# VectorE's pieces at fixed places of the attention strings, copied score tiles and twelve projection pieces in the last 64 steps

## The chip, the cores and the metric

The kernel runs on one core of a Trainium2 chip. The metric is the device time of one execution in microseconds (us). Its engines are TensorE (PE; its weight loads are shown apart as PEld), VectorE (DVE), ScalarE (ACT), GpSimd (POOL) and SyncE (SP), which here only issues DMAs. Each works through its own instructions in program order and waits on semaphores for the others.

## The reference

Two layers, each an attention block and a Fourier block (FNet) with a residual around both. S = 2048 tokens, D = 640, H = 32 heads of 20.

```python
def _A_ref(x, wqkv, wo):
    qkv = (x @ wqkv).reshape(B, S, 3, H, Dh).transpose(2, 0, 3, 1, 4)
    q, k, v = qkv[0], qkv[1], qkv[2]
    p = softmax(einsum("bhqd,bhkd->bhqk", q, k) * Dh ** -0.5)
    o = einsum("bhqk,bhkd->bhqd", p, v)
    return o.transpose(0, 2, 1, 3).reshape(B, S, D) @ wo
def _B_ref(x, dft_seq_re, dft_seq_im, dft_hid_re, dft_hid_im):
    a = einsum("bsd,ed->bse", x, dft_hid_re); b = einsum("bsd,ed->bse", x, dft_hid_im)
    return einsum("ts,bse->bte", dft_seq_re, a) - einsum("ts,bse->bte", dft_seq_im, b)
x = A_x
for layer in (0, 1):
    x = x + _A_ref(layernorm(x), A_wqkv, A_wo)
    x = x + _B_ref(layernorm(x), dft_seq_re, dft_seq_im, dft_hid_re, dft_hid_im)
```

The four DFT matrices are inputs. The kernel uses their symmetries to do a fraction of the Fourier work, and therefore compares the matrices with these symmetries while it runs (the class Check). If the comparison fails, it does everything again in a general way that is not taken here.

## The kernel before, in words

**A layer's stages.** A prologue makes the first queries and keys and half of the values. The attention sweep follows: 512 steps. A step is one group of 4 heads, one block of 512 queries and one chunk of 128 keys; 16 steps in a row (kc = 0 to 15) share an accumulator. Then `Project.run` multiplies the attention's output o with wo, adds the residual and normalizes, and `Fourier.run` does the Fourier block.

**A step.** Two score tiles (`scores`, L666): two matmuls each, side by side on TensorE's rows, into one of three PSUM tiles of 128x1024 (`psc`). ScalarE takes the exponential of each tile into an SBUF tile `e` out of a ring of 7 (L674). Then `values` (L688) adds e times v to the accumulator `acc`. The trace lists a step as 4 matmuls of L666, 8 of L688 and 2 ACTIVATEs. A score tile can be *copied*: VectorE moves it to SBUF (L671, `e<-psc`), which frees the PSUM tile, and ScalarE takes the exponential later from SBUF in place (`e<-e`).

**Fill work on TensorE.** Beside the steps TensorE makes the queries, keys and values that later heads need, in blocks (`block`, 'f'), into one PSUM tile `fill`. VectorE then works on the result: `keep` rounds it to a high part (L275), subtracts it for the low part (L263), and keeps the largest squares (L271, L272); GpSimd stores both parts. `norm` ('n') is one small matmul over these squares (L301). When no such work is left, `block` takes pieces of the projection: `Project.begin` (L1208) does the first three fifths of half a token tile's product with wo, 9 matmuls of 128x320 (L99 to L101), and VectorE adds the residual (L1215). `Project.product` (L1223) leaves out what is begun. Before, five token tiles are begun, so ten pieces.

**The order** of all instructions is written out by strings, one letter at a time (`sweep`): s a score tile, d or D a copied one (after d the exponentials that are due come out first, after D they wait for the next s), v the values of a step, f a block, n a norm, h one piece of waiting VectorE work.
- Steps below 233: DENSE strings of 8 steps (two blocks, two copied tiles); while the second half of v is made (steps 128 to 191), 4-step strings without copies. Before, neither has an h.
- Steps 233 to 408: eleven LOOSE strings (`STRING`) of 16 steps, 11 copied tiles, 12 h and 3 blocks each. Here the ring has 3 more `ex` tiles (`widen`), and `keep`'s operations are put into the list `soon` (when `defer` is set) and taken out one by one at h.
- Steps 409 to 447: no string, no block.
- Steps 448 to 511: ten strings of 5 to 8 steps (`tail`), one block each, no copied tile.

**VectorE's other work.** After each 16 steps `finish` transposes the accumulator (L697), and five operations make o in two parts (L709 to L725), which GpSimd stores (L729). Outside of the LOOSE strings all five come out at once. `compare` hands out the tasks of Check: a load of 2 x 512 KB by GpSimd's queue (L1022) into the tiles c0 and c1, then reductions and differences on VectorE (`most`, L1027; `differ`, L1031). It spreads them over the steps, not counting the 176 LOOSE ones, so that they end near step 490, at most two per step, and those of a load not before 5 steps after it (`landed`). `tasks` are the loads and splits of wo and the hidden-DFT weights.

Of the kernel before, what the change touches and what calls it, by code (L numbers as in the profile page):

```python
# [25 lines left out]
NQ = NT // 4  # L26
# [16 lines left out]
def mha_fnet_kernel(ctx, tc, x_in, wqk, wv, wo, seq, hid, nat_seq, nat_hid, out):  # L43
# [530 lines left out]
    class Attention:  # L574
        THIN = 233
        LOOSE = range(THIN, THIN + 176, 16)
        STRING = "sDhsfsDshvvshDsvvshDsfDhsvvsDsvvsDsfshDshvhvsDsvvshDsvhhvsDsnvhv"

        def __init__(s, qkv, L):
            s.a = qkv  # L580
            s.k, s.q, s.e, s.held, s.soon, s.due = {}, {}, {}, [], [], {}
# [52 lines left out]

        def widen(s):
            x = s.a.fill("wv", [3, 2, 512], F32, "ex")
            s.extra = [lambda k=k: x[:, k] for k in range(3)]
            s.ring = s.extra + s.ring
            s.a.defer = s.soon

        def narrow(s):
            s.settle()
            s.ring = [f for f in s.ring if f not in s.extra]
            s.a.defer = None

        def settle(s):
            while s.soon:
                s.soon.pop(0)()
# [44 lines left out]
        def finish(s, g, qb):  # L693
            while s.a.defer is not None and s.held:
                s.held.pop(0)()
            t0 = s.room("ofsh", [16, 32], F32, "of")
            V.transpose(t0.rearrange("p b c -> p (b c)"), s.acc)  # L697
# [36 lines left out]
        def sweep(s, shift, begin, fill=lambda n: None, plan=None, block=None, compare=lambda n: None, norm=None):  # L734
            done = calm = n = 0

            def release():
                while s.held:
                    s.held.pop(0)()

# [12 lines left out]
            while n < len(s.steps):  # L753
                opened(n)
                order = plan and plan(n)
                if order:

                    while done < n - 1:
                        s.values(done)
                        done += 1  # L760
                    t, loose = 2 * n, n in s.LOOSE
                    for k, c in enumerate(order):
                        if c in "sdD":
                            m, j = divmod(t, 2)
# [33 lines left out]
                for _ in range(count):  # L798
                    s.values(done)
                    done += 1  # L800
            for n in range(done, len(s.steps)):
                s.values(n)
            release()

        def run(s, done, project, check):

            work, tasks, later = s.a.work(), s.a.vweights(1, s.a.fill, pause=[lambda: None] * 2), list(check)
            s.work, s.blocks, s.after, s.rest, s.more, s.landed = True, 0, None, 0, False, 0


            tail, n = {}, 448
            for steps in (6, 7, 6, 8, 6, 6, 6, 6, 5, 8):
                tail[n] = {5: "sssfssvssvvsssvv", 6: "sssfssvssvssvvsssvv", 7: "sssfssvssvssvssvvsssvv",
                           8: "sssfssvssvsvssvssvssvssvv"}[steps]
                n += steps

# [3 lines left out]
            def block(n):  # L820
                if not s.work:
                    project.parts.pop(0)()
                    return
                if not s.more:
                    norm(n)
                    s.settle()
                try:
                    f = next(work)
                    s.blocks += 1
                    s.more = f is True  # L830
                    s.after = (n + (2 if n < s.THIN else 4), f) if f and not s.more else None
                    s.rest = s.after[0] + 2 if s.after else n
                except StopIteration:
                    s.work = False
                    tasks.extend(done())
# [18 lines left out]
            def plan(n):  # L854
                if n in tail:
                    return tail[n]
                if n == s.LOOSE[0]:
                    s.widen()
                if n == s.LOOSE[-1] + 16:
# [9 lines left out]
            def compare(n):  # L869


                if n < 8:
                    return
                for _ in range(2):
                    if not later or n < s.landed or (len(check) - len(later)) * (490 - len(s.LOOSE) * 16) >= (
                            n if n < s.THIN else n - len(s.LOOSE) * 16) * len(check):
# [5 lines left out]
                    task()  # L882

# [31 lines left out]
        def general(s, done, project):  # L915
# [6 lines left out]
            for f in done():  # L922
                f()
            mx = s.room("c0", [2, NT, H], F32, "mx")[:, 0]
# [38 lines left out]
    class Check:  # L963
# [65 lines left out]
        def differ(s, to, x, y, op):  # L1029

            V.tensor_tensor(y, x, y, op=op)  # L1031
            s.most(to, y)

        def compare(s, n):
# [37 lines left out]
            def hid_first():  # L1072
                t = s.t[n]
                if m:
                    for k, x in enumerate((lolo, hilo, hihi)):
                        s.most(own[0:1, k + 1:k + 2], t[x][0:1])
                s.differ(own[0:1, 0:1], t[hilo][0:1, 1:], t[hihi][0:1, 1:], same)

# [25 lines left out]
            if is_seq:  # L1104
                def halves():
                    x = s.t[n][lolo]
                    s.differ(far[:p, 4:5], x[:, 0:256], x[:, 256:512], OP.subtract if (m == 0) == (j < NQ) else OP.add)
                out.append(halves)
# [13 lines left out]
        def compare_middle(s, m):  # L1122
# [15 lines left out]
            def rest():  # L1138
                x = s.t["mid"][:, 0]
                s.differ(far[:, 1:2], x[:, :256], x[:, 256:], same)  # L1140
                s.differ(far[:, 4:5], x[:, :128], x[:, 128:256], same)

# [25 lines left out]
    class Project:  # L1168
        def __init__(s, att, src, dst):
# [3 lines left out]

            s.begun, s.parts = set(), [lambda n=n, i=i: s.begin(n, i) for n in range(5) for i in range(2)]
            s.early = {474: [lambda: s.fetch(0, 0, 1)], 486: [lambda: s.fetch(1, 0, 0)], 503: [lambda: s.fetch(0, 1, 1)]}

        def weights(s, dc):
# [5 lines left out]

            return load, lambda: split(s.w[dc][:, 0], s.w[dc][:, 1], s.raw[dc], vector=True)

# [22 lines left out]
        def begin(s, n, i):  # L1208
# [157 lines left out]
    class Fourier:  # L1366
# [9 lines left out]
        def weights(s, k):  # L1376
# [10 lines left out]
            def parts():  # L1387
                w, d = s.w[ri, c], s.deep(ri, c)
                split(w[:d, 0], w[:d, 1], s.raw["w", k][:d], vector=True)

# [305 lines left out]
    def layer(start, src, dst, general, tasks, after):  # L1696
# [14 lines left out]
        def done():  # L1711
# [11 lines left out]
            def along(k, *fs):  # L1723
                first = out[k]
                out[k] = lambda: [f() for f in (first, *fs)]
# [147 lines left out]
```

## Time and profile before

| | us |
|---|---|
| median of 3 runs | 2408.72 (2408.35 to 2409.49) |
| the profiled execution | 2408.86 |
| its span, first to last instruction | 2407.0 |
| layer 0: first score to step 448 | 82.2 to 962.4 |
| layer 0: step 448 to the first projection product of `Project.run` | 962.4 to 1085.97 |
| layer 0: the products of `Project.run` | 1085.97 to 1143.26 |
| layer 1: the same three | 1275.9 to 2157.4, to 2279.96, to 2337.25 |

All times in the views are us from the first instruction. In a view by windows each engine has its busy time, with the number of instructions that begin in the window in brackets. In a list of waits stand the total, the number of times and the longest. In a timeline row x4 means four instructions merged; what stands in square brackets is the idle time before them and what ended it.

### The profile page before, as it was taken

To read this page: it belongs to the slowest core of one execution; us is meant where nothing else is said; L and a number is where in the kernel's file an instruction comes from. 1 tells how busy PE (TensorE), PEld (TensorE's weight loads), DVE (VectorE), ACT (ScalarE), POOL (GpSimd) and SP (SyncE) were. 2 spreads that over 40 slices of the span, in tenths; PEclk is the share of its full clock that TensorE was granted. 3 is DMA by queue.
4 is the path that set the end of the run, shared out by engine and by line. 5 is a ranking of instruction groups with operands and counts; after the bars stand their busy time and mean duration, and the time that the engine had idled before them with its cause. 6 is when DMAs were issued, how large, how long until landed. Compare 5 with 4: busy or idle time off the path is not lost. (4 is left out here: it accounts for less than half of the span.)

```text
span 2407.0 us, 44028 instructions
## 1 busy us (share of the span) xinstructions
PE 2379.7 (99%) x16200; PEld 1168.9 (49%) x16200; DVE 1393.2 (58%) x2654; ACT 2091.0 (87%) x2402; POOL 553.1 (23%) x1080
## 2 busy tenths in 40 slices
PE   9999999999999999999999999999999999999998
PEld 8644445544333332339885444454443333333496
DVE  7355664367666664527774766543566666644275
ACT  5799998899999999995357999988999999999852
POOL 3022221122111112215341122211211111223143
PEclk9999999999999999999999999999999999999999
DMA  6445342223121225319673343422221212243195
GB/s 210 134 155 169 125 134 67 94 93 103 56 76 55 71 79 166 116 53 322 236 237 112 109 146 104 138 72 59 71 85 52 85 50 70 76 145 90 51 324 213
DMA packets 136704, 289.02 MB, mean 120 GB/s; under 512 B 31628, under 2 KB 56108, under 8 KB 136480
## 3 DMA queue, kind: packets, MB, share of 16 engines
q1 hardware_dynamic: 93408, 171.07, 21.9%
q0 software_dynamic: 43072, 115.06, 14.9%
q8 instruction: 130, 2.13, 0.4%
q14 instruction: 94, 0.77, 0.1%
HBM read 187.38 MB, written 92.70 MB: 116 GB/s over the span
## 5 line engine op out<-in xcount | busy, mean ns | idle before, releaser
L674 ACT ACTIVATE e<-psc 128x1024 f32<-128x1024 f32 x1586 | 1554.5, 1117 | 89.2 <-PE psc L666 87.7
L688 PE MATMUL acc<-e,v 128*32 128x512 f32 x7336 | 946.9, 599 | 1.5 <-DVE of L697 1.4
L666 PE MATMUL psc<-stq,stk 62*128 62x512 f32 x4096 | 714.4, 440 | 6.1 <-ACT e L674 3.8
L666 PEld LDWEIGHTS psc<-stq,stk 62*128 62x128 f32 x4096 | 333.3, 184 | 631.0 <-ACT e L674 408.1
L671 DVE COPY e<-psc 128x1024 f32<-128x1024 f32 x248 | 303.3, 1223 | 349.6 <-PE psc L666 331.7
L688 PEld LDWEIGHTS acc<-e,v 128*32 128x32 f32 x7336 | 204.7, 109 | 378.4 <-issue 329.5
L106 PE MATMUL pqk<-xt,wqk 128*128 128x512 f32 x1200 | 321.1, 408 | 2.9 <-DVE xt L94 0.9
L674 ACT ACTIVATE e<-e 128x1024 f32<-128x1024 f32 x248 | 302.8, 1221 | 5.0 <-DVE e L671 4.8
L729 POOL DMA_DIRECT2D o<-oh x256 | 131.7, 522 | 701.0 <-DVE oh L722 673.2
L106 PEld LDWEIGHTS pqk<-xt,wqk 128*128 128x128 f32 x1200 | 214.2, 189 | 95.7 <-issue 44.9
L674 ACT ACTIVATE ex<-psc 128x1024 f32<-128x1024 f32 x136 | 163.0, 1256 | 1.3 <-PE psc L666 1.3
L106 PE MATMUL pv<-wv,xt 128*128 128x320 f32 x960 | 151.7, 313 | 0.0
L106 PEld LDWEIGHTS pv<-wv,xt 128*128 128x128 f32 x960 | 141.0, 188 | 13.7 <-issue 10.2
L688 PE MATMUL acc<-ex,v 128*32 128x512 f32 x856 | 145.7, 598 | 0.0
L729 POOL DMA_DIRECT2D o<-ot x256 | 128.4, 508 | 16.5 <-DVE ot L725 14.5
L671 DVE COPY ex<-psc 128x1024 f32<-128x1024 f32 x78 | 95.5, 1225 | 56.5 <-PE psc L666 51.0
L697 DVE STREAM_TRANSPOSE of<-acc 128x512 f32<-128x512 f32 x64 | 45.7, 715 | 127.4 <-PE acc L688 127.4
L1027 DVE TENSOR_REDUCE far<-cq 128x1 f32<-128x512 f32 (+5 forms) x169 | 98.5, 584 | 5.7
L674 ACT ACTIVATE ex<-ex 128x1024 f32<-128x1024 f32 x78 | 101.2, 1297 | 0.0
L99 PE MATMUL py<-wo,o 128*128 128x320 f32 x320 | 101.0, 316 | 0.0
L1031 DVE TENSOR_TENSOR cq<-cq 128x512 f32<-128x512 f32 (+4 forms) x166 | 96.6, 582 | 5.7 <-DMA cq<-in_nat_seq_dram 5.6
L260 POOL DMA_DIRECT2D scrq<-hl x40 | 28.5, 713 | 310.3 <-DVE hl L263 237.3
(226 smaller groups left out, 2092.4 us busy)
## 6 DMA issues: line engine op xcount, KB each, us to landing
cq<-in_nat_seq_dram POOLq DMA_DIRECT2D x64, 512.0 KB, 5.5
scrq<-hl POOLq DMA_DIRECT2D x40, 512.0 KB, 4.0
scrk<-hl POOLq DMA_DIRECT2D x40, 512.0 KB, 3.1
stq<-scrq SPq DMA_DIRECT2D x256, 80.0 KB
stk<-scrk SPq DMA_DIRECT2D x128, 160.0 KB
chl<-matrix SPq DMA_DIRECT2D x32, 512.0 KB
o<-o SPq DMA_DIRECT2D x32, 384.0 KB
stq<-scrq SPq DMA_DIRECT2D x256, 40.0 KB
```

What stands on the lines that cost most here:

```text
L99: PE.matmul(out_ap, ah, bh, start=start, stop=False)
L106: yield lambda i=i, j=j, k=k: PE.matmul(out_ap, a[i], b[j], start=dc == 0 and k == 0, stop=dc == ND - 1 and k == 2)
L260: G.dma_start(s.scr["qk"[k]][c * 128:(c + 1) * 128, :, tb * 512:(tb + 1) * 512], hl.bitcast(F32))
L666: PE.matmul(p[:, i], s.k[g, kc // 8, j][r, kc % 8 * 128:(kc % 8 + 1) * 128], s.q[g, qb, j][r], start=True, stop=True)
L671: V.tensor_copy(e, p)
L674: s.due[n, j] = lambda: A.activation(e, e if copied in ("d", "D") else p, AF.Exp, scale=SCALE)
L688: PE.matmul(s.acc[32 * j:32 * j + 32], s.a.v[kc][:, v0:v0 + 32], s.e[n, j // 2][:, j % 2], start=kc == 0, stop=kc == NT - 1, skip_group_ch ...
L697: V.transpose(t0.rearrange("p b c -> p (b c)"), s.acc)
L729: G.dma_start(s.o[k, h * DH:(h + 1) * DH, qb * 512:(qb + 1) * 512], hl[32 * j:32 * j + DH])
L1027: V.tensor_reduce(to, x, op=OP.max, axis=AX.X, apply_absolute_value=True)
L1031: V.tensor_tensor(y, x, y, op=op)
```

## The change

1. `keep`'s operations go through `soon` in the whole sweep (`defer` is set at its start), the five of `finish` through a list `ends`, and `step` (at h) takes one from `soon`, else `ends`, else `held`, else one task of `compare`. DENSE strings get 11 h each; their letters are otherwise the same. An operation of two instructions (a comparison's difference and its reduction, the split of a weight) returns its second one, which waits for the next h. Where no string with h runs, everything is emitted at once as before.
2. `compare` counts a LOOSE step as 0.15 of a step and ends at step 441 (`pace`). A load's tasks come 4 steps after it, not 5.
3. The last 64 steps are four ENDING strings of 16 steps, each with 11 copied tiles, 16 h and 3 blocks. The ring has two more tiles there, c0 and c1, which the comparison no longer needs.
4. Twelve projection pieces: token tiles 0, 1, 2, 3, 4 and 6. The residual rows of tiles 4 to 7 are loaded earlier among the `tasks`; three loads of o stand at other steps (`early`). VectorE's add after a piece goes through `soon`.

```diff
+    def halves(hl_h, hl_l, src):
+        V.tensor_copy(hl_h, src)
+        return lambda: V.tensor_tensor(hl_l, src, hl_h.bitcast(F32), op=OP.subtract)
...
+        LAST = range(448, 512, 16)
+        DENSE = "ssdfhhhsshsvvhssvvssdfhhhhsssvvhhssnvv"
+        ENDING = "sDsvDhhsfssdvhvssdhvhvsDhsfsDsvhhvsDsvhvsDhsvhvsDhsfsDsvhvhshDshvvv"
...
-        def step(s):
-            for todo in (s.soon, s.held):
+        def step(s, other):
+            for todo in (s.soon, s.ends, s.held, [other]):
                 if todo:
-                    todo.pop(0)()
+                    rest = todo.pop(0)()
+                    if callable(rest):
+                        s.held.insert(0, rest)
                     return
...
-            pieces = s.scaled(t0, g, qb)
-            if s.a.defer is None:
-                s.held.append(lambda: [f() for f in pieces])
-            else:
-                s.held += pieces
+            s.ends += s.scaled(t0, g, qb)
...
             def release():
+                s.settle()
+                s.settle(True)
                 while s.held:
-                    s.held.pop(0)()
+                    s.whole(s.held.pop(0))
...
-                    t, loose = 2 * n, n in s.LOOSE
+                    t, loose = 2 * n, "h" in order
...
-                            s.step()
+                            s.step(lambda: compare(t // 2 - 1, True))
...
+            s.a.defer = s.soon
-            tail, n = {}, 448
-            for steps in (6, 7, 6, 8, 6, 6, 6, 6, 5, 8):
-                tail[n] = {5: "sssfssvssvvsssvv", 6: "sssfssvssvssvvsssvv", 7: "sssfssvssvssvssvvsssvv",
-                           8: "sssfssvssvsvssvssvssvssvv"}[steps]
-                n += steps
...
-                if n in tail:
-                    return tail[n]
+                if n in s.LAST:
+                    if n == s.LAST[0]:
+                        assert not later
+                        s.widen([lambda k=k: s.room(f"c{k}", [2, 512], F32, "ec") for k in range(2)])
+                    return s.ENDING
...
-                    return "sssfsssvvssvv" if whole else "ssdfsssvvssvvssdfsssvvssnvv"
+                    return "sssfsssvvssvv" if whole else s.DENSE
...
+            def pace(n):
+                m = min(n, s.THIN)
+                n -= m
+                thin = min(n, len(s.LOOSE) * 16)
+                return m + 0.15 * thin + n - thin
...
-                        s.landed = n + 5
+                        s.landed = n + 4
...
             V.tensor_tensor(y, x, y, op=op)
-            s.most(to, y)
+            return lambda: s.most(to, y)
...
-            s.begun, s.parts = set(), [lambda n=n, i=i: s.begin(n, i) for n in range(5) for i in range(2)]
-            s.early = {474: [lambda: s.fetch(0, 0, 1)], 486: [lambda: s.fetch(1, 0, 0)], 503: [lambda: s.fetch(0, 1, 1)]}
+            s.begun, s.parts = set(), [lambda n=n, i=i: s.begin(n, i) for n in (0, 1, 2, 3, 4, 6) for i in range(2)]
+            s.early = {456: [lambda: s.fetch(1, 0, 0)], 482: [lambda: s.fetch(0, 0, 1)], 511: [lambda: s.fetch(0, 1, 1)]}
...
-            V.tensor_tensor(x, p, x, op=OP.add)
+            s.att.soon.append(lambda: V.tensor_tensor(x, p, x, op=OP.add))
...
-            for k, m in ((5, 0), (6, 1)):
+            for k, m in ((5, 0), (6, 1), (9, 2), (13, 3)):
                 along(k, lambda m=m: p.load(m))
-            out += [lambda: f.edges(0)] + [lambda k=k: p.load(k) for k in (2, 3)] + [lambda: f.edges(1)]
+            out += [lambda: f.edges(0), lambda: f.edges(1)]
```

More of the change, by code (lines that the diff above doesn't have):

```diff
@@ L633, in zeros, with widen @@
             nc.sync.dma_start(s.a.shift["b"][:, 1], z[:H].bitcast(F32))
-        def widen(s):
-            x = s.a.fill("wv", [3, 2, 512], F32, "ex")
-            s.extra = [lambda k=k: x[:, k] for k in range(3)]
+        def widen(s, extra):
+            s.extra = extra
             s.ring = s.extra + s.ring
-            s.a.defer = s.soon
         def narrow(s):
@@ L643, in narrow, with settle, whole @@
             s.ring = [f for f in s.ring if f not in s.extra]
[L644 to L648, printed above, removed]
-        def step(s):
-            for todo in (s.soon, s.held):
+        def settle(s, ends=False):
+            todo = s.ends if ends else s.soon
+            while todo:
+                todo.pop(0)()
+        @staticmethod
+        def whole(f):
+            rest = f()
+            if callable(rest):
+                rest()
+        def step(s, other):
+            for todo in (s.soon, s.ends, s.held, [other]):
                 if todo:
-                    todo.pop(0)()
+                    rest = todo.pop(0)()
+                    if callable(rest):
+                        s.held.insert(0, rest)
                     return
@@ L866, in plan, with compare @@
                 if n % 4 == 1 and n + (4 if whole else 8) <= s.THIN and (whole or s.blocks % 2 == 0):
-                    return "sssfsssvvssvv" if whole else "ssdfsssvvssvvssdfsssvvssnvv"
-            def compare(n):
+                    return "sssfsssvvssvv" if whole else s.DENSE
[4 more added lines that the diff above has]
+                return m + 0.15 * thin + n - thin
+            def compare(n, one=False):
                 if n < 8:
                     return
-                for _ in range(2):
-                    if not later or n < s.landed or (len(check) - len(later)) * (490 - len(s.LOOSE) * 16) >= (
-                            n if n < s.THIN else n - len(s.LOOSE) * 16) * len(check):
+                for _ in range(1 if one else 2):
+                    if not later or n < s.landed or (
+                            len(check) - len(later)) * pace(s.LAST[0] - 6) >= pace(n) * len(check):
                         break
@@ L879, in compare @@
                     if isinstance(task, tuple):
[L880 removed]
+                        s.landed = n + 4
                         task = task[1]
[L882 removed]
+                    if one:
+                        return task()
+                    s.whole(task)
             def need(n, *keys):
@@ L1724, in along, with both @@
                 first = out[k]
-                out[k] = lambda: [f() for f in (first, *fs)]
+                def both():
+                    rest = first()
+                    for f in fs:
+                        f()
+                    return rest
+                out[k] = both
             for k, m in ((1, 0), (3, 1)):
                 along(k, lambda m=m: p.fetch(0, m, 0))
-            for k, m in ((5, 0), (6, 1)):
+            for k, m in ((5, 0), (6, 1), (9, 2), (13, 3)):
                 along(k, lambda m=m: p.load(m))
-            out += [lambda: f.edges(0)] + [lambda k=k: p.load(k) for k in (2, 3)] + [lambda: f.edges(1)]
+            out += [lambda: f.edges(0), lambda: f.edges(1)]
             return out
```

24 lines of the change are left out of this document (13 added, 11 removed).

## The prediction

> **What bounds the kernel now.** I read the page first, then the sweep by windows at the borders of its stages, then waits, groups and timeline where the change touches them.
>
> ```profile
> span 2407.0 us, 44028 instructions
> ...
> PE 2379.7 (99%) x16200; PEld 1168.9 (49%) x16200; DVE 1393.2 (58%) x2654; ACT 2091.0 (87%) x2402; POOL 553.1 (23%) x1080
> ```
>
> ```profile
> 577.70:873.70 296.00, 295.37 (x2083) 115.09 (x2079) 198.75 (x262) 296.00 (x322) 51.26 (x97) 1.00 0.22 67
> 903.00:962.40 59.40, 59.39 (x396) 17.33 (x392) 26.72 (x65) 59.40 (x66) 14.10 (x24) 1.00 0.52 167
> 962.40:1085.97 123.57, 122.01 (x870) 47.33 (x866) 47.78 (x101) 119.22 (x129) 20.59 (x38) 1.00 0.28 85
> ...
> 2157.40:2279.96 122.56, 122.38 (x873) 47.45 (x869) 40.37 (x102) 119.11 (x129) 26.19 (x50) 1.00 0.23 64
> 1085.97:1143.26 57.29, 57.29 (x392) 57.29 (x391) 42.97 (x114) 28.70 (x57) 31.33 (x75) 1.00 0.97 334
> 2279.96:2337.25 57.29, 57.29 (x393) 57.29 (x392) 43.31 (x114) 28.59 (x57) 28.19 (x75) 1.00 0.96 334
> ```
>
> A window's columns are its length, the busy time of PE, PEld, DVE, ACT and POOL, the granted clock (1.00 everywhere, so it explains nothing), the share of the DMA engines and GB/s. The page says 99% PE, but a matmul that is spread out counts as busy too, so this names no bound. The stages do:
> - The first row holds ten LOOSE strings (steps 240 to 399). ACT is busy 296.00 of 296.00 us: **ACT bounds them**, at 296.00 / 320 = 0.925 us for an exponential, or 29.60 us for a string of 32.
> - In the sweep without blocks (second row) it is ACT again, 59.40 of 59.40.
> - The next two rows are the last 64 steps of each layer with what follows until the projection. ACT idles there for 123.57 - 119.22 = 4.35 us and for 122.56 - 119.11 = 3.45 us.
> - The last two are the products of the projection. PE and its weight loads fill all of it: **PE bounds it**, and each matmul taken out is a gain.
>
> **Twelve pieces instead of ten.** 2 x 9 = 18 matmuls of each layer go from the products into the sweep.
>
> ```profile
> 1085.97:1143.26 57.29, 57.29 (x390) 57.19 (x390) 13.76 (x62) 1.00 0.97 334
> ```
>
> ```profile
> L99 PE MATMUL py<-wo,o 128*128 128x320 f32 x130 | 40.2, 309 | 0.0
> ```
>
> The first row is the same window for the tile py alone: 390 matmuls in 57.29 us are 0.147 us each (the mean of 309 ns in the second row overlaps with the next). 18 x 0.147 = 2.65 us a layer, **5.3 us** for two. Next to be late would be the data, on DMA engines that are busy 0.97 of this time. I take nothing off, because the second row has no idle time before its 130 matmuls; it is a rival below. The three loads of o that move to steps 456, 482 and 511 go through SP's queue ahead of the projection's own loads. The last of them waits for o of the steps that end at 495, whose five operations the string has at its first six h, before its middle. I count the moved loads, and the two residual loads that come earlier, at nothing: in these 64 steps the DMA engines are busy 0.28 and 0.23 of the time, which covers them. Without that cover the projection would start late by one load.
>
> **The last 64 steps.** Four ENDING strings replace ten short ones. Like LOOSE each has 32 score tiles, 11 of them copied, and 16 values.
>
> ```profile
> L674 ACT ACTIVATE e<-psc 128x1024 f32<-128x1024 f32 x129 | 120.3, 1054 | 3.3 <-PE psc L666 3.3
> ```
>
> ```profile
> PE acc L688 <- DVE of L697: 1.4, 1, 1.4
> ```
>
> ```profile
> 1075.50 9.44 ACT L674 ACTIVATE e<-psc 128x1024 f32<-128x1024 f32 x10
> ...
> 1085.97 0.42 PE L99 MATMUL py<-wo,o 128*128 128x320 f32 x1
> ```
>
> In layer 0's 4.35 us of idle ACT, 3.3 wait for score tiles (first row), and PE itself waited 1.4 us once, because the transpose that frees the accumulator stood behind comparison work on DVE (second row). The rest comes after the last exponential, which ends at 1075.50 + 9.44 = 1084.94; the projection begins 1.03 us later (last two rows). This 1.03 us stays. If the copied tiles keep ACT full as in LOOSE, 4.35 + 3.45 - 2 x 1.03 = 5.7 us can go. Reading the copies costs ACT nothing new: 119.22 / 129 = 0.924 us for each now, against LOOSE's 0.925. Does the added fill fit?
>
> ```profile
> L106 PE MATMUL pqk<-xt,wqk 128*128 128x512 f32 x150 | 42.8, 415 | 0.0
> ...
> L671 DVE COPY e<-psc 128x1024 f32<-128x1024 f32 x76 | 93.0, 1224 | 60.7 <-PE psc L666 51.9 <-ACT e L674 4.4 <-ACT ex L674 4.1
> ```
>
> These are groups of the ten LOOSE strings: their blocks take 42.8 / 10 = 4.28 us of PE a string. An ENDING string has 27 x 0.147 = 3.97 us, so PE isn't worse off. On DVE 11 copies are 11 x 1.224 = 13.5 us of 29.6, which leaves 16 us for 16 h. The bounds of the unknown: 0 us, or 0.5 us a string (8 strings, 4 us) if the nine-tile ring and the longer letters leave gaps. LOOSE is nearer, so I take 0.1 a string: 5.7 - 0.8 = **4.9 us**.
>
> [...] Read by matmul occupancy (122.38 of 122.56), the 36 matmuls would lengthen these steps by the 5.3 us that they save later.
>
> **DENSE strings with fixed places.** Their letters for PE stay; DVE's work is spread.
>
> ```profile
> 245.20:277.50 32.30, 10.63 (x64) 5.07 (x64) 4.90 (x4) 26.48 (x29) 1.00 0.43 141
> 277.50:310.90 33.40, 10.75 (x64) 5.16 (x64) 4.86 (x4) 26.55 (x29) 1.00 0.36 113
> 1307.90:1341.50 33.60, 11.21 (x66) 5.14 (x66) 4.85 (x4) 26.49 (x29) 1.00 0.37 123
> 1341.50:1375.30 33.80, 10.66 (x66) 5.11 (x66) 4.86 (x4) 26.51 (x29) 1.00 0.36 117
> ```
>
> ```profile
> PE pn L301 <- DVE sq L272: 1.3, 2, 1.0
> PE psc L666 <- ACT e L674: 1.1, 2, 0.7
> PE pqk L106 <- DVE top L302: 0.8, 1, 0.8
> PE psc L666 <- DVE e L671: 0.6, 1, 0.6
> ```
>
> ```profile
> PE pn L301 <- DVE sq L272: 0.8, 1, 0.8
> ```
>
> ```profile
> 1341.66 0.41 DVE L271 TENSOR_TENSOR sqh<-hl 128x256 bf16<-128x256 f32 x1
> ...
> 1342.90 0.29 DVE L272 TENSOR_TENSOR sq<-sq,sqh 128x256 bf16<-128x256 bf16 x1
> ...
> 1343.24 0.38 PE L301 MATMUL pn<-sq,ind 128*32 128x512 bf16 x1 [1.02 <-DVE sq L272]
> ```
>
> The four windows are 16 steps each, for the score tile: 32.30 us undisturbed, up to 33.80 where PE waits. The first list of waits is of 1275 to 1540 us: DVE's part is 1.3 + 0.8 + 0.6 = 2.7 us in layer 1. In the last rows the norm stands 1.02 us because `sq` is made in one burst with what was queued before it. In layer 0 (82 to 345 us) there is one of 0.8, so 3.5 us in all are listed; by the windows, with the restart after a wait, it is up to 1.1 + 1.3 + 1.5 = 3.9 in these three alone. With 11 places in 8 steps, `keep`'s four pieces get the four h behind the second block and the five of `finish` come singly. Bounds: 0, if new waits take their place, and 5. I take **3.0 us**, most of the listed.
>
> **What the h bring into LOOSE, and the earlier landing.** Pieces of the comparison fill empty h, and its tasks come 4 steps after their load.
>
> ```profile
> 636.90:666.50 29.60, 29.51 (x214) 11.56 (x210) 21.01 (x29) 29.60 (x34) 5.32 (x10) 1.00 0.19 58
> 696.10:725.70 29.60, 29.54 (x213) 11.27 (x209) 19.53 (x26) 29.60 (x34) 5.18 (x10) 1.00 0.30 89
> ```
>
> ```profile
> DVE ctop L1027 <- DMA cq<-in_nat_seq_dram: 23.8, 9, 8.2
> ...
> DVE ctop L1027 <- DMA cq<-in_nat_hid_dram: 11.7, 4, 5.4
> ```
>
> ```profile
> cq<-in_nat_seq_dram POOLq DMA_DIRECT2D x64, 512.0 KB, 5.5
> ```
>
> A string with 21.01 us of DVE takes the 29.60 us of one with 19.53, so a piece or two more cost nothing there. A load is two DMAs with 5.5 us to landing; 4 steps are 4 x 29.60 / 16 = 7.4 us, so most land in time. DVE already waits for 13 of them, 35.5 us in all, and while it waits the copies behind it stand, PE behind the copies, ACT behind PE. One step less is 1.85 us more for those that are late. In LOOSE fall 0.15 x 176 = 26 of the 292 steps that the comparison counts (233 + 26 + 33), a tenth of its loads, some two a layer. If one in three is late, that is one or two waits in all; bounds 0 and 4 x 1.85 = 7.4 us. I take **0.7 us lost**. In steps 409 to 447 DVE is busy 26.72 of 59.40 us, so what the comparison has left finds room.
>
> **Sum.** 5.3 + 4.9 + 3.0 - 0.7 = 12.5 us. The profiled execution took 2408.86 us (span 2407.0), 0.14 above the median of 2408.72. 2408.7 - 12.5 = **2396.2 us**. A measurement of this kernel can tell about 0.2%, 4.8 us, from no change.
>
> **The rivals.**
> - *The last 64 steps keep their length* (chance 0.16). PE or the ring, not ACT, paces ENDING, at 0.5 us a string beyond LOOSE or more: 4.9 us shrink to about 0.9, so 2400.2. For it: PE's 122.38 of 122.56. [...]
> - *The projection is bound by DMA* (0.06). Its bytes are the same and the engines busy at 0.97; then the 5.3 us come back there as waits for o: 2401.5. Against: no product waits now, at 334 GB/s. [...]
> - *Slower: pieces push the copies in LOOSE* (0.11). If in each of the 22 strings one comparison operation comes ahead of a copy that is due and its whole time reaches ACT,
>
> ```profile
> L1031 DVE TENSOR_TENSOR cq<-cq 128x512 f32<-128x512 f32 (+4 forms) x166 | 96.6, 582 | 5.7 <-DMA cq<-in_nat_seq_dram 5.6
> ```
>
>   22 x 0.582 = 12.8 us eat the whole gain; two per string, or one with a landing of 1.85 us in every third string, make 22 x 1.16 = 25.6, so 2396.2 + 25.6 = 2421.8. It decides from 12.5 / 22 = 0.57 us a string. For it: ACT has no slack there at all. Against: the two windows with 21.01 and 19.53 us of DVE.
> - *The edit does little* (0.05). The h are taken by `keep`, `finish` and tasks, the bursts come at the next release, and the pieces wait for one another: 2407.
> - *More* (0.09): all DENSE waits go (5) and ENDING needs nothing extra (5.7): 2408.7 - 5.3 - 5.0 - 5.7 = 2392.7, or a little below.
>
> **How the numbers follow.** The forecast has 0.53, between 2393 and 2400. The range 2390 to 2406 takes in the first two rivals and More, and leaves out the slower one and the little one, 0.16, and some of the tails. Faster by over 0.2% means below 2403.9: the forecast, the first two rivals and More, less their upper tails: 0.77. Within 0.2%: those tails, the little one and the weak end of the slower one: 0.14. Slower: 0.09.
>
> **What would show it.** In the new profile: the products' window 2.65 us shorter, with 372 matmuls of py and no PE wait; from step 448's first score to the first product about 121 us, ACT idle for 1 to 2; DENSE windows near 32.3 to 32.7 throughout; LOOSE strings of 29.6. LOOSE at 30.2 or more, with DVE waiting for c tiles ahead of its copies, would prove me wrong, and so would ENDING strings over 30.1 or waits for o in the products.

## The result and the profile after

The changed kernel takes **2434.11 us** (median of 4 runs, 2431.74 to 2436.88), the kernel before 2408.88 on the same chip: a ratio of **1.0105**, 95% interval 1.0088 to 1.0123. The forecast was 2396.2 with a range from 2390 to 2406. The profiled execution took 2431.85 us, 23.1 us more span than before. The page of the changed kernel, whose rows are the span and the busy time of the engines:

```profile
span 2430.1 us, 44075 instructions
...
PE 2378.8 (98%) x16200; PEld 1173.3 (48%) x16200; DVE 1497.4 (62%) x2746; ACT 2090.8 (86%) x2402; POOL 554.5 (23%) x1080
```

Its windows, with the columns of the prediction's (length, busy PE, PEld, DVE, ACT, POOL, granted clock, DMA share, GB/s):

```profile
144.90:181.30 36.40, 34.49 (x230) 15.22 (x226) 17.89 (x29) 30.09 (x33) 6.05 (x13) 0.95 0.31 99
214.00:248.80 34.80, 32.88 (x227) 13.99 (x223) 18.27 (x34) 30.06 (x33) 8.33 (x16) 1.00 0.43 134
941.70:981.80 40.10, 32.04 (x206) 9.05 (x202) 17.02 (x42) 30.39 (x34) 6.10 (x11) 0.87 0.48 142
2148.60:2184.20 35.60, 32.31 (x206) 9.13 (x202) 14.55 (x43) 30.76 (x34) 13.08 (x24) 0.90 0.36 100
981.79:1102.48 120.69, 119.82 (x888) 50.97 (x884) 77.27 (x98) 119.19 (x129) 16.01 (x32) 1.00 0.21 56
2184.21:2304.92 120.71, 119.83 (x888) 50.95 (x885) 77.28 (x98) 118.83 (x129) 16.03 (x32) 1.00 0.21 57
1102.48:1157.14 54.66, 54.66 (x377) 54.66 (x373) 42.86 (x114) 27.84 (x57) 30.23 (x71) 1.00 0.98 342
585.80:615.40 29.60, 29.59 (x212) 11.57 (x208) 20.22 (x29) 29.60 (x33) 6.75 (x12) 1.00 0.38 119
```

Read them from below. A LOOSE string still takes 29.60 us with ACT at 100%. The products take 54.66 us instead of 57.29 (in layer 1, not shown, the same), and the last 64 steps 120.7 instead of 123.57 and 122.56. Three of the forecast's terms are there. The loss is in the first four rows: 16-step windows of DENSE (steps 32 and 64) at 36.40 and 34.80 us, and the last 16 steps before 448 at 40.10 in layer 0 and 35.60 in layer 1. What PE waited for says why. Its list for the changed kernel (total, times, longest):

```profile
PE pqk L111 <- DVE wqk L91: 14.3, 8, 1.8
PE acc L702 <- DVE of L710: 9.4, 2, 8.1
PE psc L680 <- ACT e L688: 3.9, 6, 0.8
PE pflag L1180 <- DVE cmax L1175: 3.3, 1, 3.3
```

The third stood there before, with 3.8. The other three are new or have grown (the one for the accumulator was 1.4), and all end on VectorE.

**The first loss: a weight's split behind a copied tile.** The timeline of the changed kernel at the border of two DENSE strings (start, length, engine, line, operation, and in square brackets the idle time before it):

```profile
145.56 0.39 PE L306 MATMUL pn<-sq,ind 128*32 128x512 bf16 x1
...
148.67 1.23 DVE L685 COPY e<-psc 128x1024 f32<-128x1024 f32 x1 [0.20 <-PE psc L680]
149.81 0.48 DVE L91 CAST wqk<-wraw 128x640 fp32r<-128x640 f32 x1
...
150.33 0.82 DVE L94 TENSOR_TENSOR wqk<-wraw,wqk 128x640 fp32r<-128x640 f32 x1
150.35 2.93 PE L111 MATMUL pqk<-xt,wqk 128*128 128x512 f32 x6 [1.79 <-DVE wqk L91]
```

The norm (145.56, the letter n) sets off the split of the weights that the next blocks need. That is a piece of VectorE work now, and it goes into `soon`. In DENSE no h stands behind n, so the piece waits for the next string and comes out at that string's f, directly ahead of the products that read it. By then the copy of the letter d (148.67) is queued on VectorE ahead of it. PE stands 1.79 us, four times in each layer.

**The second loss: the comparison comes too late to steps 409 to 447.** The DMA issues of its natural-order loads, by the line of the load, in the kernel before and in the changed one (number, shortest/median/longest ns, first and last start):

```profile
L1022 POOL DMA_DIRECT2D cq<-in_nat_seq_dram x64: 708/734/767, 262.9 to 1607.9; - x64
```

```profile
L1042 POOL DMA_DIRECT2D cq<-in_nat_seq_dram x64: 708/728/771, 376.5 to 1678.4; - x64
```

The first comes at 376.5 instead of 262.9 us. Counted from the kernel's own order of instructions, some 142 of 175 tasks are handed out by step 409 in layer 0 where 155 are due, and some 131 of 166 in layer 1 where 147 are due. The rest follows as fast as `landed` allows. In layer 0 five loads start between steps 409 and 448, at 903.2, 917.5, 927.9, 940.0 and 961.3 us. The timeline around the fourth, in the changed kernel:

```profile
940.00 1.44 POOL L1042 DMA_DIRECT2D cq<-in_nat_seq_dram  x2 [10.53 <-DVE bound L559]
...
948.19 0.69 DVE L1047 TENSOR_REDUCE ctop<-cq 128x1 f32<-128x512 f32 x1 [6.79 <-DMA cq<-in_nat_seq_dram]
...
953.56 0.70 DVE L710 STREAM_TRANSPOSE of<-acc 128x512 f32<-128x512 f32 x1
...
954.32 1.94 PE L702 MATMUL acc<-e,v 128*32 128x512 f32 x8 [8.06 <-DVE of L710]
```

The first reduction of the load comes 4 steps after it and stands 6.79 us on VectorE until the data land. Behind it in VectorE's queue are its own followers and then the transpose that frees the accumulator (953.56). PE waits 8.06 us for that. In layer 1 the last, small loads (`middle`, eight DMAs each) do the same to the comparison's final sum, 3.3 us.

### The profile page after: what moved, and what is told of

It reads as the page before. It is cut to its first block, busy times and chain, and to the rows that moved or that the text cites. A ratio compares the mean times of both kernels' runs of the same rounds, so it can differ in the third digit from the quotient of the medians.

```text
span 2430.1 us, 44075 instructions
## 1 busy us (share of the span) xinstructions
PE 2378.8 (98%) x16200; PEld 1173.3 (48%) x16200; DVE 1497.4 (62%) x2746; ACT 2090.8 (86%) x2402; POOL 554.5 (23%) x1080
## 5 line engine op out<-in xcount | busy, mean ns | idle before, releaser
L688 ACT ACTIVATE e<-psc 128x1024 f32<-128x1024 f32 x1458 | 1449.1, 1115 | 122.6 <-PE psc L680 120.5
L702 PE MATMUL acc<-e,v 128*32 128x512 f32 x7096 | 929.8, 601 | 9.4 <-DVE of L710 9.4
L680 PE MATMUL psc<-stq,stk 62*128 62x512 f32 x4096 | 706.9, 439 | 6.1 <-ACT e L688 3.9
L685 DVE COPY e<-psc 128x1024 f32<-128x1024 f32 x316 | 386.8, 1224 | 445.6 <-PE psc L680 422.8
L688 ACT ACTIVATE e<-e 128x1024 f32<-128x1024 f32 x316 | 380.3, 1203 | 0.5 <-DVE e L685 0.4
L111 PE MATMUL pqk<-xt,wqk 128*128 128x512 f32 x1200 | 326.2, 412 | 16.5 <-DVE wqk L91 14.3
L265 POOL DMA_DIRECT2D scrk<-hl x40 | 28.2, 704 | 355.6 <-DVE hl L268 149.3
```

What stands on the lines that cost most here:

```text
L111: yield lambda i=i, j=j, k=k: PE.matmul(out_ap, a[i], b[j], start=dc == 0 and k == 0, stop=dc == ND - 1 and k == 2)
L265: G.dma_start(s.scr["qk"[k]][c * 128:(c + 1) * 128, :, tb * 512:(tb + 1) * 512], hl.bitcast(F32))
L680: PE.matmul(p[:, i], s.k[g, kc // 8, j][r, kc % 8 * 128:(kc % 8 + 1) * 128], s.q[g, qb, j][r], start=True, stop=True)
L685: V.tensor_copy(e, p)
L688: s.due[n, j] = lambda: A.activation(e, e if copied in ("d", "D") else p, AF.Exp, scale=SCALE)
L702: PE.matmul(s.acc[32 * j:32 * j + 32], s.a.v[kc][:, v0:v0 + 32], s.e[n, j // 2][:, j % 2], start=kc == 0, stop=kc == NT - 1, skip_group_ch ...
```

## The experiments

The four windows of DENSE with the split (steps 32, 64, 96 and 224) and the two before step 448 (416 and 432) carry nearly all of the loss. The time of 16 steps in us, from first score to first score, of layer 0 / layer 1:

| kernel | 32 | 64 | 96 | 224 | 416 | 432 |
|---|---|---|---|---|---|---|
| before | 33.50/33.79 | 32.49/32.49 | 33.38/33.01 | 32.31/31.57 | 29.26/29.26 | 30.18/30.17 |
| after | 36.40/36.31 | 34.79/34.79 | 36.56/36.54 | 33.88/33.87 | 30.13/29.26 | 40.11/35.60 |
| e1 | 32.69/32.69 | 32.49/32.49 | 32.76/32.76 | 31.57/31.57 | 29.86/29.25 | 40.57/35.76 |
| e2 | 34.93/36.28 | 34.79/34.75 | 36.48/36.56 | 33.81/33.83 | 29.26/29.25 | 30.19/30.19 |
| e4 | 32.69/32.69 | 32.49/32.49 | 32.76/32.76 | 31.57/31.57 | 29.25/29.25 | 30.19/30.19 |

### e1: the split right behind the norm

The list `soon` is emptied behind the norm, so the split comes out there. These lines are an excerpt.

```diff
                     f, s.after = s.after[1], None
                     f()
+                    if n < s.THIN:
+                        s.settle()
```

> One edit on the changed kernel: below step 233 the list soon is emptied right behind a norm, so that the split of the next weights comes out there and not at the next block, behind the copied tile. Theory A (the weights' split queued behind the copy makes the first block of each chunk wait): the eight waits of 1.8 us for wqk go, with the half clock that follows some of them; the 16-step windows of steps 32, 64, 96 and 224 fall from 33.9 to 36.6 us to 32.0 to 32.7, together 23 us: 2411 us. Rival R1 (the half clock comes by itself, from load or heat, and makes the waits look long): the waits become shorter but the clock is lost elsewhere, 2425 or more. Rival R2 (any of the pieces at h delays the copies, the split is only one of many): no more than 8 us gained, 2426 or more. The steps 409 to 447 stay as they are in all of them.

2409.46 us; ratio to the kernel before 1.0006 (0.9996 to 1.0015). The waits for wqk are gone and the DENSE windows are at 32.7; the ones before step 448 hardly change:

```profile
146.50:179.20 32.70, 32.70 (x230) 14.40 (x226) 17.81 (x29) 30.07 (x33) 6.05 (x13) 1.00 0.34 109
931.10:971.70 40.60, 31.76 (x206) 8.90 (x202) 17.01 (x42) 30.43 (x34) 6.20 (x11) 0.87 0.48 140
```

The first loss is the split: 24.7 us by the medians, and by the table (3.71 + 2.30 + 3.80 + 2.31) + (3.62 + 2.30 + 3.78 + 2.30) = 24.1.

### e2: no late comparison

This version leaves out the comparison's loads and tasks from step 409 on, all but the last two. These lines are an excerpt.

```diff
                     task = later.pop(0)
+                    if n >= s.LOOSE[-1] + 16 and getattr(task, "__name__", "") not in ("end", "sum"):
+                        continue
```

> One edit on the changed kernel: the comparison's tasks that would run from step 409 on are left out (loads and reductions of the last fifth of each layer's share; only the last two tasks of layer 1 run). Theory B (the comparison is 13 tasks late at step 409, catches up at one load in 6 or 7 steps, and VectorE's wait for these loads holds the transpose of the accumulator): the windows of steps 416 and 432 go back to 29.3 and 30.2 us in both layers, 16 us in all: 2418 us. Rival (these waits come from the split of wo and the hidden weights, which also run there, or from GpSimd's stores of o): no change beyond 3 us, 2431 or more. DENSE stays with its eight waits.

2422.1 us; ratio 1.0062 (1.0045 to 1.0078). The windows at step 432 come back to 30.2 with no wait of PE:

```profile
938.70:968.90 30.20, 30.20 (x204) 8.81 (x201) 5.13 (x11) 30.20 (x34) 4.20 (x8) 1.00 0.38 106
2136.70:2166.90 30.20, 30.19 (x208) 8.83 (x204) 6.38 (x18) 30.20 (x34) 4.19 (x8) 1.00 0.36 100
```

By the table that is 0.87 + 9.92 + 5.41 = 16.2 us; by the medians 12.0, with single runs of the two kernels up to 5.1 and 7.5 us apart. A part of the difference lies behind the attention: the profiled execution of e2 ends 12.35 us after VectorE's last operation, that of the changed kernel 7.74. Why stays open.

### e3: both edits

> Both edits: soon emptied behind a norm, and the comparison's tasks from step 409 on left out (a part of the comparison is not done). A and B together: 2434.1 - 23.4 - 16.2 = 2394.5 us, the granted clock back at 0.997 or more, and the spread of single runs back to about 1 us. If the two losses share a cause, or if a wait that was hidden takes their place: 2400 to 2410. If the last 64 steps and the projection owe their 10 us to the disturbed stages before them: about 2405.

2398.19 us; ratio 0.9957 (0.9941 to 0.9974). Without the two losses, and with the comparison's last part left out, the change is a gain. It takes longer than e4 below, which leaves nothing out; up to VectorE's last operation the two profiled executions differ by only 0.8 us (2382.68 and 2381.92), and e3, like e2, then ends later (11.97 us behind it, 8.90 in e4).

### e4: three h more in DENSE

Nothing is left out here; only the string is longer, by two h in its first half and one behind n.

```diff
-        DENSE = "ssdfhhhsshsvvhssvvssdfhhhhsssvvhhssnvv"
+        DENSE = "ssdfhhhsshhsvvhhssvvssdfhhhhsssvvhhssnhvv"
```

> One edit on the changed kernel, nothing left out: the DENSE string gets 14 h instead of 11, one of them right behind the norm. The split comes out at that h, and the comparison gets more places below step 233, so that it is on time at step 409 (20 tasks left and not 33). A and B: both losses go, but 20 tasks in steps 409 to 447 keep some wait there: 2395 to 2400 us. R2 (pieces at h delay the copies): three more h make DENSE slower than in the first run, 2405 or more.

2393.31 us; ratio **0.9939** (0.9922 to 0.9955), and again in e11 2394.05, 0.9936 (0.9919 to 0.9953). It is faster than both kernels, and nearly where the prediction put the change, with DENSE gaining more than was forecast and the other terms about as much. The split now stands ahead of the copy, in the timeline of this kernel at the same border:

```profile
146.53 0.47 DVE L91 CAST wqk<-wraw 128x640 fp32r<-128x640 f32 x1
147.03 0.83 DVE L94 TENSOR_TENSOR wqk<-wraw,wqk 128x640 fp32r<-128x640 f32 x1
...
148.42 2.11 PE L111 MATMUL pqk<-xt,wqk 128*128 128x512 f32 x8
148.60 1.22 DVE L685 COPY e<-psc 128x1024 f32<-128x1024 f32 x1
```

The comparison is on time at step 409 (155 tasks handed out in layer 0, 155 due), and the steps before 448 take what ACT takes:

```profile
928.20:958.40 30.20, 30.19 (x204) 8.81 (x200) 12.36 (x29) 30.20 (x34) 4.20 (x9) 1.00 0.66 211
958.40:1079.11 120.71, 119.83 (x889) 50.97 (x885) 77.26 (x98) 119.20 (x129) 15.98 (x32) 1.00 0.20 56
1079.11:1133.77 54.66, 54.66 (x377) 54.66 (x374) 42.84 (x114) 27.86 (x57) 30.24 (x71) 1.00 0.98 341
```

### e5: the last 64 steps without copied tiles

Made from e4, as are e6, e7 and e9: every d and D of ENDING becomes s.

```diff
-        ENDING = "sDsvDhhsfssdvhvssdhvhvsDhsfsDsvhhvsDsvhvsDhsvhvsDhsfsDsvhvhshDshvvv"
+        ENDING = "sssvshhsfsssvhvssshvhvsshsfsssvhhvsssvhvsshsvhvsshsfsssvhvhshsshvvv"
```

> On the version with more h (2393.3 us). Edit: in the ENDING string every d and D becomes s, so the last 64 steps have no copied score tile; nothing is left out, and the h, blocks and the two more ring tiles stay. Theory: the copied tiles keep ScalarE full, and they are what makes the last 64 steps of the two layers 4.7 us shorter; without them that comes back, 2393.3 + 4.7 = 2398, with PE or ACT waits for score tiles (about 3 us a layer) there. Rival: the gain is the new order of the letters and the wider ring, the copies add nothing: 2393.3, within 2.

2406.1 us; ratio 0.9989 (0.9979 to 0.9998), by the ratios 12 us above e4. The last 64 steps of layer 0 in e5 (layer 1 differs by 0.04 us):

```profile
958.89:1085.42 126.53, 123.39 (x889) 50.65 (x885) 26.11 (x54) 119.87 (x129) 16.00 (x32) 1.00 0.18 52
```

ACT is busy as long as with copies (119.87), but idle for 126.53 - 119.87 = 6.66 us instead of 120.71 - 119.20 = 1.51. In this order of letters the copies are what keeps ACT full, and they are worth 5.8 us a layer, more than the 2.4 a layer that the forecast gave the whole ENDING edit: without them these steps are longer than before the change.

### e6: DENSE without h, and e10: the same with a landing of 5

```diff
-        DENSE = "ssdfhhhsshhsvvhhssvvssdfhhhhsssvvhhssnhvv"
+        DENSE = "ssdfsssvvssvvssdfsssvvssnvv"
```

> On the version with more h (2393.3 us). Edit: the DENSE string of the kernel before, without h; the rest of the change stays, nothing is left out. By the count the comparison is on time at step 409 here (148 tasks of 166 done, 147 due, in layer 1), so the late comparison does not return. Theory: with enough h the spreading in DENSE is worth what the prediction's bounds gave it at most, 5 us, since the version with more h is 14.9 us below the kernel before and 5.3 + 4.7 of that are the projection and the last 64 steps: 2393.3 + 5 = 2398, and the DENSE windows go back to 33 to 33.8 us. Rival: the DENSE windows of before were long for another reason than the bursts, 2393.3.

2421.19 us; ratio 1.0054 (1.0038 to 1.0071). This was a miss: 28 us above e4 and slower than the kernel before, which has the same string. PE's waits in e6:

```profile
PE pqk L111 <- DVE top L307: 8.1, 3, 3.4
PE pn L306 <- DVE sq L273: 4.8, 1, 4.8
```

The comparison was on time, so lateness is not it. The guess was the landing of 4 steps; e10 is e6 with this line back:

```diff
-                        s.landed = n + 4
+                        s.landed = n + 5
```

> The version without h in DENSE (2421 us), with the tasks of a load 5 steps after it, not 4; nothing is left out. Theory: without h the first task of a load stands in one burst with the pieces of a norm, so a load that lands late holds the norm and PE (its long windows have 5.9 and 3.1 us of VectorE waiting for a load); one step, 2.05 us, more takes most of these waits away, and the rest is what bursts cost in the kernel before: about 2399, with no window over 34.5 us in steps 16 to 127. Rival: the landing is not it, the bursts themselves have become longer: 2415 to 2421 as before this edit.

2417.88 us; ratio 1.0034 (1.0021 to 1.0046). The guess fell: windows of 38.40 and 35.90 us are still there.

```profile
1341.30:1379.70 38.40, 34.83 (x229) 15.55 (x225) 25.44 (x50) 30.38 (x34) 6.85 (x12) 0.96 0.29 97
```

In the timeline of e10 at one of them, `top`, which the next products wait for, stands behind a comparison step that waits for its load and behind the operations that follow it:

```profile
1362.68 0.16 DVE L1078 TENSOR_TENSOR cedge<-cq 128x2 f32<-128x2 f32 x1 [2.65 <-DMA cq<-in_nat_seq_dram]
...
1364.69 0.67 DVE L307 TENSOR_REDUCE top<-pn 32x1 f32<-32x512 f32 x1
...
1365.42 3.61 PE L111 MATMUL pqk<-xt,wqk 128*128 128x512 f32 x8 [2.05 <-DVE top L307]
```

So with the rest of the change in place the h in DENSE are worth 28 us with a landing of 4 (e6 against e4) and some 20 with one of 5 (e10 against e9, below). Why the same string cost only some 6 us in the kernel before is not settled. By `pace`, 233 of 292 counted steps lie ahead of step 233 (80%), before 233 of 314 (74%): more of the comparison falls into these bursts. That was not tried by itself.

### e7: ten pieces

```diff
-s.begin(n, i) for n in (0, 1, 2, 3, 4, 6) for i in range(2)]
+s.begin(n, i) for n in range(5) for i in range(2)]
...
-                    project.parts.pop(0)()
+                    if project.parts:
+                        project.parts.pop(0)()
```

> On the version with more h (2393.3 us). Edit: ten projection pieces (token tiles 0 to 4) instead of twelve, so the last f of each layer does nothing and 18 matmuls a layer go back into the products; nothing is left out. Theory: the two pieces are hidden in the last 64 steps, the products go from 54.66 back to 57.3 us in each layer, and the time rises by 5.3 us to 2398.6. Rival: the two pieces lengthen the last 64 steps by as much as they save behind them (matmul occupancy 99%): those steps become 2.65 us shorter a layer and the time stays at 2393.3.

2399.93 us; ratio 0.9961 (0.9947 to 0.9975) against 0.9939 and 0.9936 of e4: 0.0022 x 2408.8 = 5.3 us, or 6.0 by the second. Last 64 steps and products of layer 0 in e7:

```profile
959.65:1081.30 121.65, 118.51 (x870) 48.62 (x866) 76.47 (x96) 119.37 (x129) 16.03 (x32) 0.99 0.20 54
1081.30:1138.59 57.29, 57.29 (x394) 57.29 (x391) 43.19 (x114) 28.58 (x57) 28.58 (x75) 1.00 0.97 337
```

The products are back at 57.29, and the last 64 steps are not shorter with less fill (121.65 against 120.71). The pieces are hidden there. PE's busy time did not tell how much more fits in: in e4 PE is busy for 119.83 of 120.71 us and has these two pieces in it, in e7 for 118.51 of 121.65 without the two. Of the 0.94 us by which the steps became longer 0.9 lie in the last 16 of them, where the two f without a piece stand. In all of e7 PE waits 9.2 us for score tiles, 12 times, in all of e4 3.9 us, 6 times, and the mean granted clock of the 64 steps is 0.99, in e4 1.00.

### e8: one h behind n

From the changed kernel, only the h that gives the split its place:

```diff
-        DENSE = "ssdfhhhsshsvvhssvvssdfhhhhsssvvhhssnvv"
+        DENSE = "ssdfhhhsshsvvhssvvssdfhhhhsssvvhhssnhvv"
```

> On the changed kernel (2434). Edit: one letter h more in DENSE, right behind n (12 h instead of 11); nothing is left out. The split then has a place of its own before the next string, and by the count the comparison is 5 or 6 tasks late at step 409 in layer 1 (142 of 166, 147 due) instead of 16. Theory, a threshold: steps 409 to 441 hold as many loads as fit at 14 us each (four, some 24 tasks); 24 tasks are left, 35 in the changed kernel, so no wait in them: about 2395, with the windows from step 432 at 30.2 us. Rival, in proportion: a third of the 16 us comes back, 2393.3 + 5 = 2398 to 2400, with a 4 to 5 us longer window at step 432 shared by the layers. If the split does not come out at the new h, the waits of 1.8 us stay and the time is above 2410.

2402.86 us; ratio 0.9977 (0.9967 to 0.9986). One letter undoes 31 us. The comparison is still some 11 tasks late at step 409 in layer 0 and 5 in layer 1, and the windows of steps 416 and 432, layer 0 and then layer 1, are:

```profile
899.10:931.20 32.10, 30.27 (x197) 8.59 (x193) 18.56 (x36) 29.59 (x34) 7.70 (x13) 0.95 0.39 126
931.20:966.10 34.90, 33.10 (x206) 9.40 (x202) 18.58 (x47) 30.59 (x34) 6.09 (x11) 0.90 0.62 198
2094.90:2124.20 29.30, 29.30 (x198) 8.56 (x194) 17.24 (x48) 29.30 (x34) 15.61 (x28) 1.00 0.49 155
2124.20:2154.40 30.20, 30.20 (x208) 8.84 (x204) 9.73 (x30) 30.20 (x34) 4.50 (x9) 1.00 0.37 107
```

Layer 0 loses 7.5 us and layer 1 nothing. That is neither theory whole: a threshold, but met by one layer and not the other. Layer 0 has four of the large loads there, 6 steps apart, and PE waits once for the accumulator, 1.8 us, and twice for the DMA `stq<-shiftb`, 1.7 us together, with the granted clock at 0.90 to 0.95. Layer 1 has two large loads and the two small ones, and no wait.

### e9: e4 with a landing of 5

> On the version with more h. Edit: a load's tasks come 5 steps after it as before, not 4; nothing is left out. By the count the comparison is then 3 (layer 0) and 5 (layer 1) tasks late at step 409. Theory of the prediction: the step less costs 0.7 us in all, so this is 0.7 us faster, no difference that can be seen, and VectorE's waits for the loads shrink from 30.2 us by some 10. Rival: the earlier landing is what keeps the comparison on time, and the tasks left over make waits of PE for the accumulator in steps 409 to 447 again: 3 to 7 us slower, with one window of 32 us or more there.

2398.41 us; ratio 0.9955 (0.9939 to 0.9972), beside 0.9936 of e11 on the same chip, so some 4.5 us slower than e4, though the intervals overlap a little. In the steps the difference is one window: the one at step 416 of layer 0 is 32.6 us instead of 29.25, 3.3 us more, and PE waits 2.4 us in it for the accumulator. The first score also comes 1.5 us later than in e11, which this edit does not touch. The rival was right.

```profile
900.40:933.00 32.60, 30.25 (x196) 8.57 (x193) 21.05 (x47) 29.56 (x34) 8.13 (x14) 0.95 0.44 147
```

### e11: e4 again

> The version with more h once more, on the chip of these two runs: both theories expect 0.994 times the kernel before, some 2394.

2394.05 us, told at e4.

## Why the prediction was wrong

**Right: the projection.** Forecast 5.3 us, measured 2 x (57.29 - 54.66) = 5.26. The DMA rival did not come: the engines are busy 0.98 and nothing waits for o. e7 gave the term back.

**Right: the last 64 steps.** Forecast 4.9, measured (123.57 - 120.69) + (122.56 - 120.71) = 4.73. The sentence that copies keep ACT full is shown by e5.

**Right, almost: LOOSE.** Forecast 0.7 lost, measured 0. The slower rival, pieces that push copies in LOOSE, did not occur at all.

**Wrong: the landing.** It was counted as a cost. As e9 shows, with 14 h the earlier landing is a gain, of 3.3 us by the window at step 416: with 5 steps a load's tasks come later, and PE waits 2.4 us there for the transpose that frees the accumulator. That the comparison's lateness moved a load ahead of this transpose is argued from the count, not shown apart. The prediction counted the landing's price in the stage where loads were seen to be late, not in the stage that depends on them.

**The step that failed: DENSE.** "With 11 places in 8 steps, `keep`'s four pieces get the four h behind the second block and the five of `finish` come singly. Bounds: 0, if new waits take their place, and 5." Two things were not counted. The deferred list also holds the split of the next weights, which is queued at n, behind the last h of the string; it costs 24.1 us (e1). And a new wait is not bounded at the old waits' total: it has its own size, eight times 1.79 us and what follows it. The lower bound should have been a loss: the time of what can stand ahead of the products on VectorE, a copy of 1.2 us and the split's first half of 0.5, each time that the weights change. As an estimate that is 8 x 1.7 = 13.6 us before any change of clock. The gain itself was under-forecast: with enough h the DENSE windows of e4 are 5.7 us shorter than before ((0.81 + 0.62 + 0.74) + (1.31 + 1.10 + 0.90 + 0.25), 3.0 forecast, upper bound 5). The prediction held three long windows against the 32.30 us of another; by e4 the windows have lengths of their own (32.69 at step 32, 32.76 at step 96), and seven were too long, not three.

**The other step that failed: steps 409 to 447.** "DVE is busy 26.72 of 59.40 us, so what the comparison has left finds room." This read a share of busy time (of steps 416 to 447) as a capacity. By the timeline, what limited the work was not VectorE's time but the one pair of tiles c0 and c1: load, landing, reductions, next load, one after the other, with VectorE standing in order while a load lands, 6.79 us at the longest wait of layer 0. e2 takes out the loads and their tasks together, so it shows the cost of the late comparison and not which part of it is the limit. The prediction also took it that the comparison is on time there; it was 13 to 16 tasks late. By the code, 16 steps of DENSE have 22 h, of which `keep`'s pieces take 12 or 15, the split one and those of `finish` 5, all ahead of the comparison, whose pace asks for 9 to 10 tasks there. It cost 16.2 us by the windows (e2); e4 removes it by three more h.

The sum of the terms as measured: -5.3 - 4.7 - 5.7 + 24.1 + 16.2 = +24.6 us, against 23.1 more span; the first score came 1.6 us earlier in this execution than in the one before.

## What to carry to other kernels

When work is moved from "at once" to "at the next free place", list for each piece the place it will really get and its first reader, and count the places against all who take them; a piece without a place before its reader costs the whole queue ahead of it. Work with the lowest priority in such a list runs late without a sign until a stage where it must be done. Setting the whole operations of a burst apart made this kernel faster with 14 places in a string (0.9939, against 1.0054 without any) and not with 11 (1.0105).

## What the runs showed of the hardware

In the trace of the changed kernel the granted clock is 0.50 in six stretches of the sweeps. They start at 151.00, 287.54, 949.72, 1359.32, 1495.85 and 2175.11 us and last 3.41 us each, but for the third with 10.24 and the last with 6.83. The later ones start 40, 234, 354, 394 and 593 times 3.413 us behind the first. Windows of 3.41 us, counted from the start of the first stretch, first around the wait of 1.79 us from 148.56 to 150.35, then around the equal one from 217.68 to 219.47:

```profile
147.59:151.00 3.41, 1.62 (x9) 0.78 (x8) 3.01 (x4) 2.80 (x3) 0.00 (x0) 1.00 0.01 2
151.00:154.41 3.41, 3.29 (x9) 2.17 (x10) 3.02 (x7) 0.08 (x1) 0.65 (x2) 0.50 0.45 129
154.41:157.83 3.42, 3.42 (x30) 1.16 (x32) 0.00 (x0) 3.02 (x4) 3.37 (x7) 1.00 0.50 146
215.86:219.27 3.41, 1.82 (x15) 0.50 (x7) 2.19 (x3) 2.71 (x4) 0.00 (x0) 1.00 0.77 255
219.27:222.69 3.42, 3.09 (x14) 1.83 (x14) 3.21 (x8) 1.10 (x2) 0.00 (x0) 1.00 0.36 101
```

The first wait lies whole in one of these windows, and the next window has half the clock; the second is cut by a border, 1.59 us of it in one window, and the clock stays at 1.00. The other six waits of 1.79 us in this trace are alike: the three that lie whole in one window (from 284.81, 1357.01 and 1493.15 us) are followed by a window at 0.50, the three that a border cuts (from 556.29, 1426.02 and 1764.11 us) by none. A wait with such a stretch cost 3.6 to 3.8 us in its 16 steps, one without 2.3 (the changed kernel against e1, in the table). In e2, with waits of the same total (14.3 us, eight times), the 16 steps from step 32 have a mean clock of 1.00 in layer 0 and take 34.93 us, and in layer 1 0.95 and 36.28 us. This is what two traces have; what makes the clock fall is not shown.

The wait of 8.06 us begins at 946.26. The clock is at 0.50 from 949.72, still inside the wait, to 959.96, 10.24 us in all; PE starts again at 954.32. The wait of 3.28 us in layer 1 ends at 2176.63 and has 6.83 us of half clock, from 2175.11:

```profile
946.31:949.72 3.41, 0.00 (x0) 0.00 (x0) 0.69 (x1) 2.14 (x3) 0.00 (x0) 1.00 0.97 323
949.72:959.96 10.24, 5.64 (x24) 1.40 (x24) 9.23 (x24) 1.94 (x2) 2.98 (x6) 0.50 0.15 44
2175.11:2181.94 6.83, 5.31 (x24) 1.33 (x26) 1.44 (x8) 2.37 (x3) 0.00 (x0) 0.50 0.00 0
```
